# Local attention and channel mix in one kernel: GpSimd left out of tile arithmetic in the first units, one unit's scores split by tile, a longer strict list for TensorE

## The chip, the cores and the metric

The kernel runs on one core of a Trainium2 chip. The metric is the device time of one execution in microseconds (us); the figure for a kernel is the median of its runs. Beside the timed runs one execution is recorded by the hardware profiler; its span goes from the first to the last instruction of the program, and its own device time is a little longer.

Engines go by the profile's short names: PE is TensorE's matmul side and PEld its weight load, DVE is VectorE, ACT is ScalarE, POOL is GpSimd, SP is the engine whose queue issues all DMAs here. "L666" is line 666 of the kernel before.

## What is computed

A chunked local attention over 4 batches, 8 heads, 768 positions and 64 elements a head is followed by a channel mix over the 512 joined channels. All in fp32:

```python
for c in range(nc):                      # 24 chunks of 32 queries
    ...
    k_full = np.concatenate([mem_k, k_ctx], axis=2)   # 8 memory keys + 16 left + 32 + 8 right
    v_full = np.concatenate([mem_v, v_ctx], axis=2)
    scores = scale * np.matmul(q_c, k_full.transpose(0, 1, 3, 2))
    ...                                  # softmax over the 64 keys -> a
    out[:, :, c_start:c_end] = np.matmul(a, v_full)
...
xk = mu_k * x + (1.0 - mu_k) * x_prev    # x: attention output, x_prev: one position earlier
xr = mu_r * x + (1.0 - mu_r) * x_prev
k = np.maximum(xk @ w_k, 0.0)            # 512 -> 1024
v = k * k @ w_v                          # 1024 -> 512
r = 1.0 / (1.0 + np.exp(-(xr @ w_r)))    # 512 -> 512
return (r * v)
```

## The kernel before

**Tiling.** The 3072 positions are 24 tiles of 128 and 12 units of two tiles (256 positions). A unit u passes these steps on TensorE; each has a short name, used in the list below and in the text:

- `s u.c`: the scores, a matmul for each pair of heads, chunk and half (L371). Unit 0 does its two tiles as two operations (s0.0, s0.1); every other unit does both tiles as one, named s u.0. VectorE, ScalarE and VectorE again make the softmax of it: maximum (L384), subtraction (L389), exponential (L395), sum and reciprocal (L399 to L401), and the normalizing multiplication (L405).
- `t i`: four transposes of tile i's probabilities (L443). ScalarE or VectorE copies them into a block layout (L243 or L245).
- `a i`: the product with the values (L460). The result is copied into xT, the unit's transposed x.
- `h u.f`, four to a unit: xk times w_k (L666). For unit 0 these are eight "rows" instead, h0.k.c, one for each 128 rows k of w_k and each tile c (L641), so that each can start when its piece of w_k has come.
- `g u.c`: xr times w_r, one for each tile (L592; L584 for unit 0), followed by the sigmoid.
- `v u.c.half`: k squared times w_v (L740; L729 for unit 0), followed by the multiplication with the sigmoid (L762) and the store of the output (L765).

From unit 1 on, the channel mix splits each fp32 factor into a rounded high part (`xh`, `kh`, the weight tiles) and a low part (`xl`, `kl`, `wl`), and multiplies high by high, high by low and low by high. Unit 0 multiplies whole fp32 words. The low part of a weight is `T["w"] - high`, L299, one instruction on 128 x 1024 elements, once for each of ten weight pieces (4 of w_k, 2 of w_r, 4 of w_v). The low part of an input is L568. Before them stands the mixing: the difference of neighbouring positions (`df`, L542), then for m = 1 (gate) and m = 0 (w_k) four multiply-adds on 128 x 256 elements (L552).

**The order of the work.** The whole kernel is written as a list of operations (`Op`), each with one or several engines on which it may run, what it depends on, the buffer slots that it takes and uses, and a due time. `te_order` turns the string `LEAD` and, after it, a regular pattern for each unit into a sequence for TensorE with due times; `dues` passes due times back to all operations that these depend on. `turn` then places operations one after another on the engine and at the time where one can start first; due times break ties and, from the second turn on, weigh a tenth. `order` does three turns; each takes as its goals the starts that the turn before it gave. While fewer than `STRICT` operations of all engines are placed, TensorE may take only the next of its sequence; after that it may take a later one if that can start earlier. The loop at the end writes the instructions in the planned order, so on the chip each engine takes its instructions in that order; warm-up matmuls (L790) fill TensorE's planned pauses ahead of the first key row.

An operation with alternatives is made with `either`, such as `either(dve=(1.15, True), pool=(2.4, True))`; the numbers are planned costs, and the flag marks operations that are planned never to overlap between VectorE and GpSimd ("port"). GpSimd stands as an alternative in the normalizing multiplication (L415), the weights' low part (L309), the difference (L544), the input's low part (L573), the squaring (L707) and the low part of the square (L712).

**Buffers that matter here.** Score tiles and raw weights share five SBUF buffers ("big"), value tiles have two ("vw"); in PSUM there is one buffer for scores, two for transposes and value products ("tp") and four for the channel mix ("m"). A load into such a buffer is issued on SP's queue when its last user is done.

Of the kernel before, what the change touches and what calls it, by code (L numbers as in the profile page):

```python
# [27 lines left out]
NEG = -3.0e38  # L28
TINY = 2.0**-112
LOOK = 400  # L30
STRICT = 80
EASE = 0.1
TURNS = 3
LEAD = "s0.0 s0.1 t0 t1 a0 a1 h0.0.0 h0.0.1 h0.1.0 h0.1.1 s1.0 h0.2.0 h0.2.1 h0.3.0 h0.3.1 g0.0 t2 t3 g0.1 a2 a3 v0.0.0 s2.0 v0.0.1 v0.1.0 v0.1.1 h1.0 h1.1 h1.2 h1.3 g1.0 g1.1 t4 t5 a4 a5"
UTOK = 256
QPU = UTOK // P
QKW = NPAIR * NJ * (CHUNK + NK)
# [41 lines left out]
class Plan:  # L79
# [5 lines left out]
        self.bufs = bufs  # L85

    def op(self, alts, fn, deps=(), new=(), use=(), due=1e9):
        if isinstance(alts, tuple):
            alts = [alts]
        o = Op([(a + (False,))[:3] for a in alts], fn, deps, new, use, due)  # L90
        o.seq = len(self.ops)
        self.ops.append(o)
        return o

# [95 lines left out]
def local_attention__then__channel_mix(  # L190
# [47 lines left out]
    op = plan.op  # L238
    T = {}
# [4 lines left out]
        else:  # L244
            e.tensor_copy(dst, src)  # L245

    def either(**alts):
        return [(n, *alts[n]) for n in alts]

    qts = [(b, i) for b in range(B) for i in range(NQT)]  # L250
    units = [(b, u * UTOK) for b in range(B) for u in range(S // UTOK)]
# [1 line left out]
    due = te_order()  # L253
# [76 lines left out]
    xslot, pslot = {}, {}  # L330
    NG = 2 * QPU * NPAIR

    def scores(u):


        ts = range(u * QPU, (u + 1) * QPU)
        es = Slot("e")

        def grid(a, c, n):
            return a.rearrange("p (h c r) k -> p h c r k", h=2, c=QPU)[:, :, c : c + n].rearrange(  # L340
                "p h c r k -> p h (c r) k"
            )

        def f_load(t):
            b, i = qts[t]
            a = T["qk", t] = sb("big", [P, QKW], f"qk{t}")
            nc.sync.dma_start(a, qk[b, i])

        def part(c, n, prev, first):


            cs = range(c, c + n)
            G = NPAIR * n
            key = (u, c)

            def s4():
                return T["s", key].rearrange("p (h g k) -> p h g k", h=2, k=NK)[:, :, :G]

            def f_s():
                T["s", key] = ps("s", f"s{u}_{c}", QPU)  # L360
                s5 = s4().rearrange("p h (c r) k -> p h c r k", c=n)
                nq = NPAIR * NJ * CHUNK
                for d in cs:
                    a = T["qk", ts[d]]
                    q4 = a[:, :nq].rearrange("p (r j q) -> p r j q", r=NPAIR, j=NJ)
                    k4 = a[:, nq:].rearrange("p (r j k) -> p r j k", r=NPAIR, j=NJ)
                    for r in range(NPAIR):
                        for j in range(NJ):
                            for h in range(2):
                                z = slice(64 * h, 64 * h + 64)  # L370
                                nc.tensor.matmul(  # L371
                                    s5[CHUNK * j : CHUNK * (j + 1), h, d - c, r, :], q4[z, r, j, :], k4[z, r, j, :],
                                    start=True, stop=True,
                                )

            def f_max():
                s5 = s4().rearrange("p h (c r) k -> p h c r k", c=n)
                for d in cs:
                    if qts[ts[d]][1] == 0:
                        nc.vector.memset(s5[0:CHUNK, :, d - c, :, 0:LEFT], NEG)  # L380
                    if qts[ts[d]][1] == NQT - 1:
                        nc.vector.memset(s5[P - CHUNK : P, :, d - c, :, LEFT + CHUNK : LEFT + CHUNK + RIGHT], NEG)
                mx = T["mx", key] = sb("sm", [P, 2, G], f"mx{u}_{c}")
                nc.vector.reduce_max(mx, s4(), axis=AX.X)  # L384

            def f_sub():
                if first:
                    T["e", u] = sb("e", [P, NG, NK], f"e{u}")
                nc.vector.tensor_sub(  # L389
                    grid(T["e", u], c, n), s4(), T["mx", key].unsqueeze(3).to_broadcast([P, 2, G, NK])  # L390
                )

            def f_exp():
                e = grid(T["e", u], c, n)
                nc.scalar.activation(e, e, AF.Exp, scale=SCALE)  # L395

            def f_sum():
                sm = T["sum", key] = sb("sm", [P, 2, G], f"sum{u}_{c}")
                nc.vector.reduce_sum(sm, grid(T["e", u], c, n), axis=AX.X)  # L399
                nc.vector.tensor_scalar_add(sm, sm, 1e-9)  # L400
                nc.vector.reciprocal(sm, sm)  # L401

            def f_norm(g):
                e = grid(T["e", u], c, n)
                g.tensor_mul(e, e, T["sum", key].unsqueeze(3).to_broadcast([P, 2, G, NK]))  # L405

            w = n / QPU
            s1, m1, m2 = Slot("s"), Slot("sm"), Slot("sm")
            ds = due["s", u, c]
            o_s = op(("pe", 0.1 + 1.5 * w), f_s, [l[d] for d in cs] + [prev], new=[s1], use=[qs[d] for d in cs], due=ds)  # L410
            o_m = op(("dve", 0.1 + 1.05 * w), f_max, [o_s], new=[m1], use=[s1], due=ds + 4)
            o_b = op(("dve", 0.1 + 1.05 * w), f_sub, [o_m], new=[es] if first else [], use=[s1, m1] + [es] * (not first), due=ds + 5.5)
            o_e = op(("act", 0.15 + 0.85 * w), f_exp, [o_b], use=[es])
            o_u = op(("dve", 0.5 + 1.05 * w), f_sum, [o_e], new=[m2], use=[es])
            o_n = op(either(dve=(0.1 + 1.05 * w, True), pool=(2.2 * w, True)), f_norm, [o_u], use=[es, m2])  # L415
            if u == 0 and c == QPU - 1:
                prior["abs"].deps.append(o_e)
                prior["join"].deps.append(o_n)
            return o_s, [o_n] * n

        qs = [Slot("big") for _ in ts]
        l = [op(("dma", 2.1), lambda t=t: f_load(t), new=[x]) for t, x in zip(ts, qs)]
        o_s, done = prior.get("s"), []
        step = 1 if u == 0 else QPU
        for c in range(0, QPU, step):
            o_s, o_n = part(c, step, o_s, c == 0)
            done += o_n
        prior.update(s=o_s)
        return done, es
# [105 lines left out]
    def prep(u):  # L535
# [5 lines left out]
            d = T["df", u] = sb("x4", [P, KT, UTOK], f"df{u}")  # L541
            e.tensor_sub(d, x[:, :, 1:], x[:, :, :UTOK])  # L542

        o_d = op(either(dve=(1.15, True), pool=(2.0, True)), f_df, deps, new=[ds], use=[xslot[u]])  # L544
        for m in (1, 0):
            last = m == 0

            def f_mix(m=m, last=last):
                d = T["df", u]
                f = T["xf", u, m] = d if last else sb("x4", [P, KT, UTOK], f"xf{u}")  # L550
                for k in range(KT):
                    nc.vector.scalar_tensor_tensor(  # L552
                        f[:, k], d[:, k], mu_sb[:, m, k : k + 1], T["xT", u][:, k, :UTOK], ALU.mult, ALU.add
                    )

            def laid(m=m):
                f = T["xf", u, m]
                return f if m else f.rearrange("p k (n t) -> p t k n", t=2)

            shape = [P, KT, UTOK] if m else [P, 2, KT, UTOK // 2]  # L560

            def f_hi(e, m=m, laid=laid, shape=shape):
                h = T["xh", u, m] = sb(f"xh{m}", shape, f"xh{u}_{m}", F32R)
                copy(e, h, laid())

            def f_lo(e, m=m, laid=laid, shape=shape):
                l = T["xl", u, m] = sb(f"xl{m}", shape, f"xl{u}_{m}", F32R)
                e.tensor_sub(l, laid(), T["xh", u, m].bitcast(F32))  # L568

            fs, hs, ls = ds if last else Slot("x4"), Slot(f"xh{m}"), Slot(f"xl{m}")  # L570
            o_d = op(("dve", 1.75, True), f_mix, [o_d, o_mu], new=[] if last else [fs], use=[ds, xslot[u]])
            o_h = op(either(act=(0.97,), dve=(0.61, True)), f_hi, [o_d], new=[hs], use=[fs])
            o_l = op(either(dve=(1.15, True), pool=(2.4, True)), f_lo, [o_h], new=[ls], use=[fs, hs])  # L573
            mix[u, m] = (o_h, o_l, hs, ls)

    def channel_mix(u):
# [81 lines left out]
        for f in range(FT // 2):  # L658
# [45 lines left out]
                dh = due["h", u, f]  # L704
                o1 = op(("pe", BLOCK), f_s1, list(mix[u, 0][:2]) + wdeps(wk_hl, range(KT)), new=[s], use=list(mix[u, 0][2:]), due=dh)
            oa = op(either(act=(0.5,), dve=(0.61,)), f_relu, [o1], new=[kf], use=[s], due=dh + BLOCK + 1.5)
            ob = op(either(act=(0.54,), dve=(0.62, True), pool=(1.23, True)), f_sq, [oa], use=[kf])  # L707
            if is_whole(u, "v"):
                ks.append((ob, None, kh, kh))
                continue  # L710
            o2 = op(either(act=(0.54,), dve=(0.35, True)), f_hi, [ob], new=[kh], use=[kf])
            o3 = op(either(dve=(0.62, True), pool=(1.23, True)), f_lo, [o2], new=[kl], use=[kf, kh])  # L712
            ks.append((o2, o3, kh, kl))

        for c in range(QPU):
# [68 lines left out]
    with tc.manual_schedule():  # L784
        for o in plan.order():
            if o.eng == "pe":
# [2 lines left out]
                    warm = warm or ps("m", "warm")  # L789
                    nc.tensor.matmul(warm[:, :P], zero_sb, zero_sb, start=True, stop=True)  # L790
                busy = o.end
            if len(o.alts) > 1:
                o.fn(engines[o.eng])
            else:
                o.fn()
# [48 lines left out]
```

## Time and profile before

| what | value |
|---|---|
| median of 3 runs | 403.51 us (403.37 to 405.76) |
| the profiled execution's own time | 403.4 us |
| its span | 401.6 us |
| TensorE busy in the span | 393.3 us, 4506 matmul instructions |
| VectorE, ScalarE, GpSimd busy | 264.3, 189.1, 8.8 us |
| read from HBM, written | 42.01 MB, 6.29 MB |
| granted TensorE clock | 1.00 |

How to read it: a busy TensorE in the profile includes the warm-up matmuls and modelled ends of pipelined matmuls. An fp32 matmul appears as two matmul instructions. Timeline rows show the start, the length from the first to the last instruction of a merged group, the engine, the line, the tiles written and read, the count, and in brackets the idle time before the group and what ended it; "issue" there means that the profile shows nothing that the engine waited for. In a table by stage each engine's busy time in that stage is followed by its instruction count in brackets. A row of a DMA queue shows packets, megabytes, and the packets' time as a share of 16 engines' time in the window.

### The profile page before, as it was taken

Reading aid. Unit: us, or ns where it says so; the run is one execution under the profiler, and the core shown is the slowest. Engines: PE = TensorE matmul, PEld = TensorE weight load, DVE = VectorE, ACT = ScalarE, POOL = GpSimd, SP = SyncE. Lnnn points to the kernel's source line nnn. Section 1 sums busy time; section 2 is a strip of 40 time slices with the busy share of each in tenths; the row PEclk is TensorE's granted clock in tenths of the full one; section 3 lists DMA queues with packets and bytes.
Section 4 is the critical chain, followed back from the end, with each engine's and each line's share of the span. In section 5 each row is a group of like instructions: output and inputs, shape, how many; then the busy total and the mean of one; then the engine's idle time right before and its main releaser. Section 6 shows DMA issues by size and latency. Waiting matters only on the chain.

```text
span 401.6 us, 9978 instructions
## 1 busy us (share of the span) xinstructions
PE 393.3 (98%) x4506; PEld 352.0 (88%) x4506; DVE 264.3 (66%) x378; ACT 189.1 (47%) x271; POOL 8.8 (2%) x15
## 2 busy tenths in 40 slices
PE   8989998999999999999999999999999999999996
PEld 8988546988988998998998998998998998998995
DVE  2899899876396397397297288288378378377121
ACT  1657978661534435436436346255254354342250
POOL 2100130000000000000000000000000000000000
PEclk9999999999999999999999999999999999999999
DMA  8999925520052042133134134132130120100101
GB/s 317 421 368 387 414 95 205 243 106 26 28 192 98 28 155 113 52 124 141 52 112 154 52 107 158 54 107 80 54 106 2 54 105 3 54 2 0 52 2 52
DMA packets 12905, 48.93 MB, mean 122 GB/s; under 512 B 1472, under 2 KB 1600, under 8 KB 12352
## 3 DMA queue, kind: packets, MB, share of 16 engines
q1 hardware_dynamic: 12864, 48.31, 32.0%
q8 instruction: 35, 0.57, 0.6%
q14 instruction: 6, 0.05, 0.0%
HBM read 42.01 MB, written 6.29 MB: 120 GB/s over the span
## 4 chain that ended last, share of the span: by engine, by line
PE 95%; DVE 4%; issue 1%
PE ph L666 29%; PE pv L740 29%; PE pr L592 14%; PE px L460 6%; PE s L371 4%; PE ph L641 4%; PE warm L790 3%; PE pt L443 2%; PE pv L729 2%; PE pr L584 2%; DVE wl L299 1%; DVE xl L568 1%; DVE o L762 0%; DVE df L552 0%; DVE mx L384 0%
## 5 line engine op out<-in xcount | busy, mean ns | idle before, releaser
L666 PE MATMUL ph<-xh,wk 128*128 128x256 f32 x352 | 98.5, 280 | 0.0
L666 PE MATMUL ph<-xl,wk 128*128 128x256 f32 x352 | 96.8, 275 | 0.0
L666 PE MATMUL ph<-xh,wl 128*128 128x256 f32 x352 | 96.8, 275 | 0.0
L681 ACT ACTIVATE kf<-ph 128x512 f32<-128x512 f32 x39 | 23.1, 598 | 98.8 <-PE ph L666 98.8
L666 PEld LDWEIGHTS ph<-xh,wk 128*128 128x128 f32 x352 | 67.5, 192 | 1.0
L666 PEld LDWEIGHTS ph<-xl,wk 128*128 128x128 f32 x352 | 67.5, 192 | 0.3
L740 PE MATMUL pv<-wv,kh 128*128 128x512 f32 x176 | 67.7, 384 | 0.0
L666 PEld LDWEIGHTS ph<-xh,wl 128*128 128x128 f32 x352 | 67.6, 192 | 0.0
L740 PE MATMUL pv<-wl,kh 128*128 128x512 f32 x176 | 66.7, 379 | 0.0
L740 PE MATMUL pv<-wv,kl 128*128 128x512 f32 x176 | 66.7, 379 | 0.0
L698 DVE TENSOR_TENSOR kl<-kf,kh 128x512 fp32r<-128x512 f32 x44 | 29.5, 688 | 51.5 <-ACT kh L243 51.5
L762 DVE TENSOR_TENSOR o<-pv,sg 128x512 f32<-128x512 f32 x24 | 16.6, 691 | 37.8 <-PE pv L740 34.2
L740 PEld LDWEIGHTS pv<-wv,kh 128*128 128x128 f32 x176 | 33.3, 189 | 5.0
L740 PEld LDWEIGHTS pv<-wv,kl 128*128 128x128 f32 x176 | 33.3, 189 | 4.7
L740 PEld LDWEIGHTS pv<-wl,kh 128*128 128x128 f32 x176 | 33.3, 189 | 4.2
L592 PE MATMUL pr<-wr,xl 128*128 128x512 f32 x88 | 33.5, 380 | 0.4 <-DVE xl L568 0.4
L592 PE MATMUL pr<-wl,xh 128*128 128x512 f32 x88 | 33.4, 380 | 0.0
L592 PE MATMUL pr<-wr,xh 128*128 128x512 f32 x88 | 33.4, 379 | 0.0
L243 ACT CAST xh<-df 128x1024 fp32r<-128x1024 f32 x9 | 13.7, 1522 | 29.0 <-DVE df L552 29.0
L460 PEld LDWEIGHTS px<-aTz,vw 128*64 128x64 f32 x768 | 23.5, 138 | 2.8 <-issue 1.0
L460 PE MATMUL px<-aTz,vw 128*64 128x64 f32 x768 | 25.2, 224 | 0.4 <-issue 0.4
L245 DVE COPY aTz<-pt 64x512 f32<-64x512 f32 x21 | 14.6, 694 | 16.2 <-ACT aTz L243 10.9
(66 smaller groups left out, 566.2 us busy)
## 6 DMA issues: line engine op xcount, KB each, us to landing
qk<-in_qk_dram SPq DMA_DIRECT2D x24, 768.0 KB, 5.8
vw<-in_vw_dram SPq DMA_DIRECT2D x24, 512.0 KB, 4.8
out_dram<-o SPq DMA_DIRECT2D x24, 256.0 KB, 2.0
raw<-in_w_k_dram SPq DMA_DIRECT2D x4, 1024.0 KB, 9.8
raw<-in_w_v_dram SPq DMA_DIRECT2D x4, 1024.0 KB, 10.1
raw<-in_w_r_dram SPq DMA_DIRECT2D x2, 1024.0 KB, 7.7
id_sb<-in_ident_dram SPq DMA_DIRECT2D x1, 64.0 KB, 5.5
mu_sb<-in_mu_dram SPq DMA_DIRECT2D x1, 4.0 KB, 11.8
```

Source lines behind the costliest of these rows:

```text
L243: e.copy(dst, src)
L245: e.tensor_copy(dst, src)
L371: nc.tensor.matmul(s5[CHUNK * j : CHUNK * (j + 1), h, d - c, r, :], q4[z, r, j, :], k4[z, r, j, :], start=True, stop=True,)
L460: nc.tensor.matmul(p3[64 * h : 64 * h + 64, 2 * g : 2 * g + 2, CHUNK * j : CHUNK * j + CHUNK], v[:, g, h, j, :], a[:, h, g, j, :], start=True,
L592: nc.tensor.matmul(pairs(p), x[:, k, c * P : (c + 1) * P], woven(w), start=(k + n == 0), stop=(k == KT - 1 and n == 2),)
L641: nc.tensor.matmul(p[:, i * UTOK + c * P : i * UTOK + (c + 1) * P], T["w", id(wk_hl[0]), k][:, fc], T["xf", u, 0][:, k, z], start=(i + k + ...
L666: nc.tensor.matmul(pairs(p[:, i * UTOK : (i + 1) * UTOK]), w[:, fc], x[:, :, k].rearrange("p t n -> p n t"), start=(k + n == 0), stop=(k = ...
L681: e.activation(r, T["ph", u, f], AF.Relu)
L698: e.tensor_sub(l, T["kf", u, f], T["kh", u, f].bitcast(F32))
L740: nc.tensor.matmul(pairs(p), x[:, tc_], woven(w), start=(f + n == 0), stop=(f == FT - 1 and n == 2))
L762: nc.vector.tensor_mul(o, p, sg)
L790: nc.tensor.matmul(warm[:, :P], zero_sb, zero_sb, start=True, stop=True)
```

## The change

1. `either` leaves GpSimd out unless its first argument is true; the five uses within units give `u > 2`, and the weights' low part (L309) gives nothing. An operation that now has one engine left is still told which engine that is (`fixed`).
2. Unit 1's scores become two TensorE operations, one for each tile. Both write the same PSUM buffer; the softmax behind them stays one piece for both tiles.
3. `LEAD` is changed: s1.0 goes one key row earlier, s1.1 follows behind the next row; t4 and t5 go from behind g1.1 to between h1.1 and h1.2, a4 and a5 to between h1.2 and h1.3.
4. `STRICT` goes from 80 to 230 placed operations.

```diff
-STRICT = 80
+STRICT = 230
...
-LEAD = "s0.0 s0.1 t0 t1 a0 a1 h0.0.0 h0.0.1 h0.1.0 h0.1.1 s1.0 h0.2.0 h0.2.1 h0.3.0 h0.3.1 g0.0 t2 t3 g0.1 a2 a3 v0.0.0 s2.0 v0.0.1 v0.1.0 v0.1.1 h1.0 h1.1 h1.2 h1.3 g1.0 g1.1 t4 t5 a4 a5"
+LEAD = "s0.0 s0.1 t0 t1 a0 a1 h0.0.0 h0.0.1 h0.1.0 s1.0 h0.1.1 s1.1 h0.2.0 h0.2.1 h0.3.0 h0.3.1 g0.0 t2 t3 g0.1 a2 a3 v0.0.0 s2.0 v0.0.1 v0.1.0 v0.1.1 h1.0 h1.1 t4 t5 h1.2 a4 a5 h1.3 g1.0 g1.1"
...
     def op(self, alts, fn, deps=(), new=(), use=(), due=1e9):
-        if isinstance(alts, tuple):
+        fixed = isinstance(alts, tuple)
+        if fixed:
             alts = [alts]
...
-        o.seq = len(self.ops)
+        o.seq, o.fixed = len(self.ops), fixed
...
-    def either(**alts):
-        return [(n, *alts[n]) for n in alts]
+    def either(late=False, **alts):
+        return [(n, *alts[n]) for n in alts if n != "pool" or late]
...
-            def f_s():
-                T["s", key] = ps("s", f"s{u}_{c}", QPU)
+            def f_s(ds):
+                if ds[0] == c:
+                    T["s", key] = ps("s", f"s{u}_{c}", QPU)
...
-                for d in cs:
+                for d in ds:
...
-            o_s = op(("pe", 0.1 + 1.5 * w), f_s, [l[d] for d in cs] + [prev], new=[s1], use=[qs[d] for d in cs], due=ds)
+            o_s = prev
+            for g in [[d] for d in cs] if u == 1 else [list(cs)]:
+                first_s = g[0] == c
+                o_s = op(
+                    ("pe", 0.1 + 0.75 * len(g)), lambda g=g: f_s(g), [l[d] for d in g] + [o_s],
+                    new=[s1] * first_s, use=[s1] * (not first_s) + [qs[d] for d in g], due=due["s", u, g[0]],
+                )
...
-            o_n = op(either(dve=(0.1 + 1.05 * w, True), pool=(2.2 * w, True)), f_norm, [o_u], use=[es, m2])
+            o_n = op(either(u > 2, dve=(0.1 + 1.05 * w, True), pool=(2.2 * w, True)), f_norm, [o_u], use=[es, m2])
...
-            if len(o.alts) > 1:
+            if not o.fixed:
                 o.fn(engines[o.eng])
             else:
                 o.fn()
```

The uses at L544, L573, L707 and L712 get `u > 2` in the same way as the normalizing multiplication.

More of the change, by code (lines that the diff above doesn't have):

```diff
@@ L542, in f_df @@
             e.tensor_sub(d, x[:, :, 1:], x[:, :, :UTOK])
-        o_d = op(either(dve=(1.15, True), pool=(2.0, True)), f_df, deps, new=[ds], use=[xslot[u]])
+        o_d = op(either(u > 2, dve=(1.15, True), pool=(2.0, True)), f_df, deps, new=[ds], use=[xslot[u]])
         for m in (1, 0):
@@ L572, in prep @@
             o_h = op(either(act=(0.97,), dve=(0.61, True)), f_hi, [o_d], new=[hs], use=[fs])
-            o_l = op(either(dve=(1.15, True), pool=(2.4, True)), f_lo, [o_h], new=[ls], use=[fs, hs])
+            o_l = op(either(u > 2, dve=(1.15, True), pool=(2.4, True)), f_lo, [o_h], new=[ls], use=[fs, hs])
             mix[u, m] = (o_h, o_l, hs, ls)
@@ L706, in channel_mix @@
             oa = op(either(act=(0.5,), dve=(0.61,)), f_relu, [o1], new=[kf], use=[s], due=dh + BLOCK + 1.5)
-            ob = op(either(act=(0.54,), dve=(0.62, True), pool=(1.23, True)), f_sq, [oa], use=[kf])
+            ob = op(either(u > 2, act=(0.54,), dve=(0.62, True), pool=(1.23, True)), f_sq, [oa], use=[kf])
             if is_whole(u, "v"):
@@ L711, in channel_mix @@
             o2 = op(either(act=(0.54,), dve=(0.35, True)), f_hi, [ob], new=[kh], use=[kf])
-            o3 = op(either(dve=(0.62, True), pool=(1.23, True)), f_lo, [o2], new=[kl], use=[kf, kh])
+            o3 = op(either(u > 2, dve=(0.62, True), pool=(1.23, True)), f_lo, [o2], new=[kl], use=[kf, kh])
             ks.append((o2, o3, kh, kl))
```

## The prediction

> **What bounds the kernel now.** I read the top of the page first, then the span cut into stages, and last the timeline around each wait of TensorE.
>
> ```profile
> span 401.6 us, 9978 instructions
> PE 393.3 (98%) x4506; PEld 352.0 (88%) x4506; DVE 264.3 (66%) x378; ACT 189.1 (47%) x271; POOL 8.8 (2%) x15
> ```
> ```profile
> core 0: us, PE busy (x) PEld busy (x) DVE busy (x) ACT busy (x) POOL busy (x), PEclk, DMA share, GB/s
> 0.00:18.60 18.60, 16.91 (x282) 15.84 (x282) 10.35 (x21) 7.29 (x11) 3.54 (x10) 1.00 0.90 364
> 18.60:27.99 9.39, 9.39 (x197) 9.06 (x196) 8.73 (x17) 6.05 (x14) 0.00 (x0) 1.00 0.99 397
> 27.99:29.27 1.28, 0.00 (x0) 0.00 (x0) 1.28 (x3) 0.70 (x1) 0.00 (x0) 1.00 0.79 218
> 29.27:61.40 32.13, 32.13 (x309) 19.69 (x308) 29.47 (x37) 25.70 (x33) 4.98 (x2) 1.00 0.76 300
> 61.40:69.20 7.80, 6.36 (x165) 5.54 (x165) 7.80 (x8) 6.22 (x9) 0.00 (x0) 1.00 0.49 164
> 69.20:401.60 332.40, 328.53 (x3558) 301.88 (x3556) 206.68 (x298) 143.17 (x207) 0.32 (x3) 1.00 0.23 82
> ```
> TensorE is the bound. Up to 18.6 us it mostly passes time with warm-up matmuls; after that it works without a gap, but for one gap of 1.28 us and 1.44 us in the stage from 61.40 (the 3.87 us missing in the last stage lie behind its last matmul). Its clock is 1.00 throughout. The change moves TensorE's instructions and takes none away, so what can be won after 18.6 us is about 1.28 + 1.44 = 2.7 us, 0.7% of the span. The waits stand in brackets in the timeline (start, duration, engine, line); in the stage from 61.40 there are two:
>
> ```profile
> 48.54 5.06 POOL L299 TENSOR_TENSOR wl<-w,wk 128x1024 fp32r<-128x1024 f32 x2 [30.79 <-ACT wk L243]
> 48.88 5.79 DVE L552 SCALAR_TENSOR_TENSOR xf<-df,mu_sb,xT 128x256 f32<-128x256 f32 x4
> 51.00 10.57 PE L729 MATMUL pv<-w,kf 128*128 128x512 f32 x24
> 57.30 1.66 DVE L552 SCALAR_TENSOR_TENSOR df<-df,mu_sb,xT 128x256 f32<-128x256 f32 x4
> 61.24 1.22 DVE L405 TENSOR_TENSOR e<-e,sum 128x1024 f32<-128x1024 f32 x1
> 62.38 1.22 DVE L299 TENSOR_TENSOR wl<-w,wk 128x1024 fp32r<-128x1024 f32 x1
> 62.61 1.07 PE L443 MATMUL pt<-id_sb,e 128*128 128x128 f32 x8 [1.03 <-DVE e L405]
> 63.51 1.22 DVE L568 TENSOR_TENSOR xl<-df,xh 128x1024 fp32r<-128x1024 f32 x1
> 64.65 1.22 DVE L299 TENSOR_TENSOR wl<-w,wk 128x1024 fp32r<-128x1024 f32 x1
> 65.78 0.69 DVE L762 TENSOR_TENSOR o<-pv,sg 128x512 f32<-128x512 f32 x1
> 68.80 0.48 PE L592 MATMUL pr<-wr,xl 128*128 128x512 f32 x1 [0.40 <-DVE xl L568]
> ```
> Both of TensorE's waits there are for VectorE: the transposes t4 and t5 wait 1.03 us for unit 2's normalized softmax (L405), then the gate product g1.0 waits 0.40 us for the low part of its input (L568). The same four mixing instructions of VectorE take 5.79 us while GpSimd subtracts, and 1.66 us when it doesn't. So the two subtractions that GpSimd took over hold VectorE up by 5.79 - 1.66 = 4.13 us, and VectorE then has no rest until both of TensorE's waits are over (7.80 of 7.80 us busy from 61.40 on).
>
> **The change part by part.** *GpSimd.* Its 15 instructions hold only two on whole tiles, the two at L299 above; the others are fills and one small scaling. So taking it off the list for units 0 to 2 and for the weights moves these two and nothing else. On VectorE such a one follows the last after 1.13 us (62.38 to 63.51): it gains 4.13 us and takes on 2 x 1.13 = 2.26, and is free 1.87 us earlier from the mixing on. For TensorE that is worth at most its two waits. The norm would end at about 62.4 - 1.9 = 60.5, ahead of 61.58 (62.61 - 1.03), when the value product is done: 1.03 us gone. The gate's input is ready at 68.75 - 1.87 = 66.9, and TensorE, 1.03 us earlier, asks for it at 68.40 - 1.03 = 67.4: 0.40 us gone. Without any new order this part gives -1.43 us; the "fixed" flag and the alternatives that were never taken cost nothing.
>
> *The strict list.* TensorE now goes from the value product straight to h1.0 and h1.1, then t4, t5, h1.2, a4, a5, h1.3, g1.0, g1.1, v1.0.0, s3.0, g2.0. Its step lengths (start, duration, count; h and g stand in pairs):
>
> ```profile
> 99.66 5.36 PE ph L666 x48
> 108.57 2.02 PE px L460 x64
> 113.46 2.59 PE pv L740 x12
> 116.06 1.41 PE s L371 x89
> 120.26 5.18 PE pr L592 x24
> ```
> At 61.6 h1.0 must have four low parts of w_k and its input's two parts. VectorE's work for it, from 48.88: two mixings (2 x 1.66), four subtractions (4 x 1.13) and the input's low part (1.13), 9.0 us, to about 57.9, if the list's earlier dates put these ahead of unit 2's softmax: 3.7 us of cover. The softmax follows: max, subtract, exponential, sum and norm stand in the present trace between 54.90 and 62.4 with 1.58 and 0.61 us of other work inside, 5.3 us; from 57.9 it is done by about 64, and t4 comes at 61.6 + 5.36 = 67.0. g1.0 comes at 61.6 + 10.72 + 1.0 + 2.0 = 75.3, with three more operations (3.4 us) to do. Last, g2.0 needs unit 2's mixed input:
>
> ```profile
> 81.84 2.09 PE L460 MATMUL px<-aTz,vw 128*64 128x64 f32 x64
> 89.07 1.23 DVE L568 TENSOR_TENSOR xl<-xf,xh 128x1024 fp32r<-128x1024 f32 x1
> 83.03 1.26 SPq L437 DMA_DIRECT2D vw<-in_vw_dram  x2
> 66.94 2.06 SPq L347 DMA_DIRECT2D qk<-in_qk_dram  x4
> ```
> Today that is ready at 90.3, 6.4 us after a5 ends at 83.9. In the new list a5 ends at 72.6, and g2.0 comes at 75.3 + 5.2 + 2.6 + 1.4 = 84.5, so 11.9 us are there for 6.4. The cover gone, TensorE would wait one for one. Queued behind a blocked head are all of its later matmuls, and the output stores behind those; up to its 230th placed operation no other TensorE step may step in. Of the DMAs, the loads at L437 reuse the buffers of a4 and a5 and go out some 11 us earlier on SP's queue, for steps at 108.57; s3.0, moved from 63.6 to about 83, gives its two buffers back 20 us later, so part of the L347 loads comes then, for s4.0 at 116. With 32 us for a load that takes 13.6 us at the worst (next fence), nothing waits. The list is worth nothing on top of the 1.43 us.
>
> *The second unit's scores.* Their rows and the gap behind them:
>
> ```profile
> 18.63 7.41 PE L641 MATMUL ph<-xf,w 128*128 128x128 f32 x64
> 25.97 1.48 PE L371 MATMUL s<-qk 64*32 64x64 f32 x128
> 27.39 0.60 PE L641 MATMUL ph<-xf,w 128*128 128x128 f32 x3
> 29.27 6.97 PE L641 MATMUL ph<-xf,w 128*128 128x128 f32 x61 [1.28 <-issue]
> ```
> ```profile
> q8 instruction: 35, 0.57, 0.6%
> ...
> q8 instruction: 1, 0.02, 33.5%
> ...
> qk<-in_qk_dram SPq DMA_DIRECT2D x1, 768.0 KB, 13.6
> ```
> ```profile
> raw<-in_w_r_dram SPq DMA_DIRECT2D x1, 1024.0 KB, 7.8
> ```
> The gap lies inside a key row, with no new operand. I read it as instruction delivery: 2 x 4506 instructions came in 35 packets (the page's first q8 row), 257 each; and in the window from 26.8 to 27.0 stands the second q8 row, a packet that takes 33.5% of 16 x 0.2 us, 1.07 us, and so lands at about 28, as the gap begins. At key rows TensorE uses 122 instructions in 6.97 us; the scores use 256 in 1.48. That is inferred, not shown. The tile-wise split puts a key row (1.85 us) between the halves. The two tiles' loads (issued from 7.01, 13.6 us to landing) are there at 20.6 and some 2 us later, ahead of the new 24.1. But the instructions ahead of the gap's place are the same in either order, so TensorE gets there at 27.99 either way; only the request can go out earlier. If it goes out when TensorE comes to the block's first instruction, 8 instructions into the scores (26.0), it now comes 40 into them (24.1 + 40 x 1.48/256 = 24.3), 1.7 us earlier, and the 1.28 us are gone. If it goes out 40 or more instructions ahead, nothing moves: 0. The bad end: a block that takes as long as the data then in flight, 7.8 us, lands at 32.1, a gap of 4.1 us, 2.8 more than now. So -1.28 to +2.8; I take half of the gain, -0.6, since the packet of today came quickly and nothing slower is seen to be asked for. The Trainium skill ("Runtime: NRT & Kernel Launch", Instruction fetch mechanics) says that blocks of 256 instructions are fetched while the present one runs and that this is hidden, since an engine issues more slowly than the blocks come; the block size agrees with the rows, "hidden" would leave the gap another cause, and the sum would then be -1.43, 402.0 us.
>
> *Sum*, against the profiled execution's own 403.4 us (span 401.6 and 1.8 around it; the median of the runs is 403.51, 0.1 above): 403.4 - 1.03 - 0.40 - 0.6 = 401.4 us.
>
> **The rivals.** (1) The wait moves to h1.0: VectorE still serves unit 2's softmax ahead of the four subtractions and the input's low part. Present order with new costs: done at 65.8 - 4.13 + 2.26 = 63.9; h1.0 reads the last w_k part at its 12th of 24 matmuls, 1.2 us after 61.6, so TensorE waits 1.1 us at the head of a list that lets neither t4 nor s3.0 by. For it speaks that VectorE does the softmax first today; against it that the list gives h1.0 the earlier date. 403.4 - 1.43 + 1.1 = 403.1 us. (2) Slower: the instruction block asked for in the middle of the scores stands behind data transfers; place: the first matmuls after s1.1; price: up to 2.8 us. It decides from a landing at 29.27 + 1.43 = 30.7 us on. For it: DMA share 0.99 in that stage, and 7.8 us for data; against it: today's packet. 403.4 - 1.43 + 2.8 = 404.8 us. (3) The change does not do what it says on TensorE's side: the waits go through GpSimd's two instructions alone and the gap stays, 402.0 us; this lies in the forecast's own range. (4) The front shortens as well: up to 18.6 us TensorE has slack, but the list's first nine entries are the same, so I see no step that would.
>
> **How the numbers follow.** Forecast with both VectorE waits gone, 400.7 (whole gap gone) to 402.0 (gap stays): 0.63. Rival 1: 0.15. Rival 2: 0.15, of which 0.06 is for delays several times as long, past 1%. Rival 4: 0.07, mostly small. The range reaches from 400.5, just under the forecast's best, to 404.4, most of rival 2. About 1%, 4 us, is what a measurement of this kernel can tell from no change: the most that the trace has to give is 2.7 us, so faster by over 1% needs rival 4: 0.04; slower by over 1%: 0.06; within: 0.90.
>
> **What would show it right or wrong.** Right: GpSimd without L299; every four instructions at L552 in about 1.66 us; TensorE without a wait from 61 to 85 us, h1.0 right behind the value product; the last matmul some 2 us earlier. The gap behind the scores shorter or gone confirms the half taken; unchanged at 1.28 us, the sum is 402.0. Wrong: a wait of ph L666 for wl or xl (rival 1), a longer gap at L641 or between the halves of L371 (rival 2), a wait of g2.0 for xl, or a first key row that no longer starts near 18.6 us.

## The result and the profile after

The changed kernel takes 401.73 us (median of 6 runs), the kernel before beside it 403.89 us; the ratio of the two is 0.9938, with a 95% interval from 0.9918 to 0.9957. That is 2.2 us or 0.6% faster, and within the 1% that the prediction set as its bound. The profiled execution took 401.57 us against 403.4, 1.8 us less; the account below is made on it. One of the six runs of experiment x3 below took 671.6 us at a granted clock of 0.558, against 0.998 or more in its other five, and is left out of its ratio.

The top of the page, and the stages up to 69.20 us, cut where this kernel has its gap and its waits would be:

```profile
span 399.8 us, 9971 instructions
...
PE 392.7 (98%) x4506; PEld 352.1 (88%) x4506; DVE 263.3 (66%) x381; ACT 188.7 (47%) x270; POOL 3.4 (1%) x13
```
```profile
0.00:18.60 18.60, 16.54 (x282) 15.42 (x282) 10.44 (x21) 7.29 (x11) 3.04 (x10) 1.00 0.91 363
18.60:28.35 9.75, 9.71 (x195) 9.21 (x196) 8.78 (x17) 6.65 (x14) 0.00 (x0) 1.00 1.00 391
28.35:29.43 1.08, 0.00 (x0) 0.00 (x0) 1.08 (x2) 0.29 (x1) 0.00 (x0) 1.00 0.96 387
29.43:61.70 32.27, 32.27 (x311) 20.02 (x311) 29.67 (x38) 26.02 (x33) 0.00 (x0) 1.00 0.83 316
61.70:69.20 7.50, 7.50 (x70) 7.50 (x69) 7.07 (x9) 5.23 (x8) 0.00 (x0) 1.00 0.68 247
```
GpSimd has two instructions less, and TensorE is busy throughout the stage from 61.70, where it lacked 1.44 us. The gap behind unit 1's scores is still there, with 1.08 us. The timeline of VectorE and TensorE (start, duration, engine, line; L560 is the old L552, L300 the old L299, L451 the transposes, L649 the key rows, L373 the scores, L674 the old L666):

```profile
49.03 1.67 DVE L560 SCALAR_TENSOR_TENSOR xf<-df,mu_sb,xT 128x256 f32<-128x256 f32 x4
...
57.76 2.48 DVE L300 TENSOR_TENSOR wl<-w,wk 128x1024 fp32r<-128x1024 f32 x2
...
64.26 1.22 DVE L407 TENSOR_TENSOR e<-e,sum 128x1024 f32<-128x1024 f32 x1
```
```profile
18.63 5.62 PE L649 MATMUL ph<-xf,w 128*128 128x128 f32 x48 [0.41 <-DVE xf L533]
24.19 0.86 PE L373 MATMUL s<-qk 64*32 64x64 f32 x64
24.98 2.05 PE L649 MATMUL ph<-xf,w 128*128 128x128 f32 x16
26.96 0.86 PE L373 MATMUL s<-qk 64*32 64x64 f32 x64
27.75 0.60 PE L649 MATMUL ph<-xf,w 128*128 128x128 f32 x3
29.43 6.97 PE L649 MATMUL ph<-xf,w 128*128 128x128 f32 x61 [1.09 <-issue]
...
66.90 1.04 PE L451 MATMUL pt<-id_sb,e 128*128 128x128 f32 x8
```
The four mixing instructions take 1.67 us instead of 5.79. The last low part of w_k is ready at 60.24 and the softmax at 65.48; TensorE needs them at about 62.8 and 66.9.

From the chain that ended last, the start of unit 2's h2.0, up to which both kernels have done the same work (before: 99.66, in the prediction):

```profile
97.84 5.36 PE ph L674 x48
```
So 1.82 us are won by then, the whole of it. The path up to the end of the gap became longer: the first key row starts at 18.63 in both, and the gap ends at 29.43 instead of 29.27. From there to h2.0 it is 68.41 us instead of 70.39, 1.98 us less. Most of that, 1.77 us, is the two waits for VectorE, as x1 shows below; the other 0.21 us come with the new order of the steps.

### The profile page after: what moved, and what is told of

The parts are those of the page before. It is cut to its first block, busy times and chain, and to the rows that moved or that the text cites. A ratio compares the mean times of both kernels' runs of the same rounds, so it can differ in the third digit from the quotient of the medians.

```text
span 399.8 us, 9971 instructions
## 1 busy us (share of the span) xinstructions
PE 392.7 (98%) x4506; PEld 352.1 (88%) x4506; DVE 263.3 (66%) x381; ACT 188.7 (47%) x270; POOL 3.4 (1%) x13
## 4 chain that ended last, share of the span: by engine, by line
PE 94%; DMA 3%; SPq 1%; ACT 0%; issue 0%; DVE 0%; DVEq 0%
PE ph L674 30%; PE pv L748 29%; PE pr L600 14%; PE px L468 6%; PE s L373 4%; PE ph L649 4%; PE pv L737 4%; DMA raw<-in_w_k_dram 3%; PE pt L451 2%; PE pr L592 2%; ACT w L286 0%; SPq L445 0%; SPq L348 0%; SPq L270 0%; DVE o L770 0%
## 5 line engine op out<-in xcount | busy, mean ns | idle before, releaser
L674 PE MATMUL ph<-xh,wk 128*128 128x256 f32 x352 | 99.0, 281 | 0.0
L674 PE MATMUL ph<-xl,wk 128*128 128x256 f32 x352 | 96.8, 275 | 0.0
L674 PE MATMUL ph<-xh,wl 128*128 128x256 f32 x352 | 96.8, 275 | 0.0
L674 PEld LDWEIGHTS ph<-xh,wk 128*128 128x128 f32 x352 | 67.5, 192 | 1.2 <-issue 0.2
L674 PEld LDWEIGHTS ph<-xl,wk 128*128 128x128 f32 x352 | 67.5, 192 | 0.5 <-DVE e L391 0.2
L674 PEld LDWEIGHTS ph<-xh,wl 128*128 128x128 f32 x352 | 67.6, 192 | 0.0
L397 ACT ACTIVATE e<-e 128x1024 f32<-128x1024 f32 (+1 forms) x13 | 12.9, 993 | 28.5 <-DVE e L391 28.5
```

What stands on the lines that cost most here:

```text
L674: nc.tensor.matmul(pairs(p[:, i * UTOK : (i + 1) * UTOK]), w[:, fc], x[:, :, k].rearrange("p t n -> p n t"), start=(k + n == 0), stop=(k = ...
```

## The experiments

Ten kernels. Each ratio is to the kernel before on the same chip and comes from the timed runs; a span is that of the one profiled execution, and spans of one kernel's runs differ by up to 1.1 us in most of these kernels and by 2.2 to 4.0 us in four (x3, y2, y3, y4).

| kernel | span, us | ratio (95% interval) |
|---|---|---|
| the changed kernel | 399.8 | 0.9938 (0.9918 to 0.9957) |
| x1, only the engine of two instructions | 400.0 | 0.9956 (0.9944 to 0.9968) |
| x2, changed, GpSimd back | 400.7 | 0.9969 (0.9957 to 0.9981) |
| x3, changed, wide warm-up | 398.7 | 0.9920 (0.9902 to 0.9937) |
| x4, changed, scores in one piece | 400.1 | 0.9946 (0.9934 to 0.9958) |
| y1, changed, two warm-up matmuls fewer | 400.0 | 0.9952 (0.9938 to 0.9967) |
| y2, before, wide warm-up | 402.6 | 1.0006 (0.9991 to 1.0022) |
| y3, GpSimd out, old list | 400.8 | 0.9974 (0.9959 to 0.9990) |
| y4, wide warm-up, one piece, t later | 399.1 | 0.9931 (0.9915 to 0.9948) |
| z1, y4 with two operations exchanged | 398.9 | 0.9912 (0.9899 to 0.9926) |
| z2, the new list alone | 401.2 | 0.9972 (0.9961 to 0.9982) |

**x1: only the engine of the two subtractions.** Every engine keeps its old order.

```diff
-                o.fn(engines[o.eng])
+                o.fn(engines["dve" if o.eng == "pool" else o.eng])
```


> The kernel before with every engine's order as it was; only the two subtractions at L299 that GpSimd did go to VectorE, at their old places in the plan. Theory A (VectorE's lateness, made by GpSimd, is what TensorE waited for): the four mixing instructions at L552 take 1.66 us again, the norm is ready by 60.6 us and the gate's input by 67, both of TensorE's waits are gone although its sequence is the old one, the gap of 1.28 us stays, span 401.6 - 1.8 = 399.8 us. Rival B (the new sequence is what wins): in the old sequence the waits stay within 0.3 us of 1.03 and 0.40, span 401.3 to 401.6 us.

Measured: 400.0 us. VectorE, then TensorE's first waits on its list of waits:

```profile
49.16 1.67 DVE L552 SCALAR_TENSOR_TENSOR xf<-df,mu_sb,xT 128x256 f32<-128x256 f32 x4
...
59.67 1.23 DVE L405 TENSOR_TENSOR e<-e,sum 128x1024 f32<-128x1024 f32 x1
```
```profile
PE ph L641 <- issue: 1.2, 1, 1.2
PE warm L790 <- DVE zero_sb L232: 1.0, 1, 1.0
PE px L460 <- POOL xT L472: 0.4, 1, 0.4
```
Both waits for VectorE are gone in the old sequence. What they cost is the time from the gap's end to h2.0, in the chain that ended last (the second row is cut by the view's end at 100 us):

```profile
29.49 6.97 PE ph L641 x61
98.11 1.90 PE ph L666 x17
```
That is 68.62 us instead of 70.39, so 1.77 us, for listed idle times of 1.43. The span falls by 1.6 us only, because here the first key row starts 0.3 us later (18.89 us instead of 18.63), though the instructions ahead of it are the same. Theory A holds and B falls: two instructions on another engine are worth 0.44%, against 0.62% for the whole change, and the two intervals overlap.

**x2: the changed kernel with the two subtractions on GpSimd.**

```diff
+    slow = [wdone[id(wk_hl[0]), k][1] for k in range(2)]
...
-                o.fn(engines[o.eng])
+                o.fn(engines["pool" if o in slow else o.eng])
```


> The changed kernel in its own order, but its first two low parts of w_k go back to GpSimd. Theory A: the first four mixing instructions take about 5.8 us again, VectorE is late by 4.13 - 2.26 = 1.9 us, h1.0 still finds its operands (about 62.1 us against 62.9 us), the softmax for t4 is late (about 67.4 against 66.9 us), so one wait of 0.5 us at t4 and a span of about 400.4 us. Rival B (the sequence carries the gain, VectorE's time doesn't matter): 399.8 us, no wait. Rival C (GpSimd alone carries it and the sequence hides nothing): 401.5 us, with waits of 1.4 us or more.

Measured: 400.7 us. VectorE's mixing and TensorE's wait:

```profile
49.07 5.77 DVE L560 SCALAR_TENSOR_TENSOR xf<-df,mu_sb,xT 128x256 f32<-128x256 f32 x4
```
```profile
PE pt L451 <- DVE e L407: 0.8, 1, 0.8
```
The 5.8 us are back, h1.0 doesn't wait, t4 waits 0.8 us (expected 0.5). So the new sequence hides a part of VectorE's lateness, and B and C both fall.

**z2: the new list and the strict count alone.**

```diff
-STRICT = 80
+STRICT = 230
...
-LEAD = "... v0.1.1 h1.0 h1.1 h1.2 h1.3 g1.0 g1.1 t4 t5 a4 a5"
+LEAD = "... v0.1.1 h1.0 h1.1 t4 t5 h1.2 a4 a5 h1.3 g1.0 g1.1"
```


> The kernel before with the new list and the strict count of 230 alone (scores in one piece, GpSimd allowed as before; the planner then gives GpSimd other work: one input's low part, one low part of w_r, one low part of a square, 2.5 us each or less). Theory A (what counts is whether VectorE is held up ahead of TensorE's needs): GpSimd's work comes later, where the list leaves more time, so part of the two waits stays: span 400.0 to 401.0 us. Rival B (the list alone carries the gain): 399.8 us. Rival C (GpSimd's removal alone does): 401.3 us or more.

Measured: 401.2 us, a little above A's range and just under C's; this execution was one of the longest of its eight, whose median span of 400.9 us lies in A's range. The gap has 1.9 us here instead of 1.3, and t4 waits 0.7 us. The plan now gives GpSimd other work, and VectorE is held up again, a subtraction of 1.22 us taking 3.39:

```profile
56.90 2.54 POOL L568 TENSOR_TENSOR xl<-xf,xh 128x1024 fp32r<-128x1024 f32 x1 [39.62 <-ACT xh L243]
```
```profile
57.13 3.39 DVE L568 TENSOR_TENSOR xl<-df,xh 128x1024 fp32r<-128x1024 f32 x1
```
GpSimd's subtraction ends at 59.44 and VectorE's at 60.52, 1.08 us later, about what it takes alone. The list alone is worth 0.28% (1.1 us). From the gap's end (29.95) to h2.0 (99.28) it is 69.33 us: the list without GpSimd's removal wins 1.06 of the 1.98 us there.

**y3: GpSimd's removal alone, as written,** with the planner free to reorder: the `either` and `fixed` hunks of the change, nothing else.

> The kernel before with the change's first part alone, as written: GpSimd is no alternative in units 0 to 2, list and strict count as before; the planner then also finds another order on TensorE by itself. Theory A: no wait for VectorE is left, the gap stays, span 399.8 us. Rival B (the new list carries the gain): 401.3 us or more.

Measured: 400.8 us, a miss by 1.0 for A, though no wait for VectorE's softmax or low parts is left. The planner put t4 and t5 between and behind the gate products with a4 right after them, which costs a new wait (a4 for a copy, 0.3 us), the first key row starts some 0.3 us later, and the gap is 1.7 us. This run doesn't separate the theories well; x1, with the order held, does.

**x4: the changed kernel with unit 1's scores in one piece.**

```diff
-            for g in [[d] for d in cs] if u == 1 else [list(cs)]:
+            for g in [[d] for d in cs] if u == -1 else [list(cs)]:
...
-LEAD = "... h0.1.0 s1.0 h0.1.1 s1.1 h0.2.0 ..."
+LEAD = "... h0.1.0 h0.1.1 s1.0 h0.2.0 ..."
```


> The changed kernel with unit 1's scores in one piece at the old place, the rest as changed. Theory A with D: the gap comes back to about 1.28 us (0.2 more), but a switch into the scores and one out of them less save about 0.36 us; span 399.6 us, that is the split costs 0.15 us. Rival F (the split is worth its half of the gap, as the prediction took it): 400.4 us.

Measured: 400.1 us and 0.9946. The gap is 1.5 us, and the key rows start about 0.3 us later. Against the changed kernel's 0.9938 that is no difference that these intervals can tell: neither the 0.15 us that I expected the split to cost nor F's 0.6 us gain is shown.

**x3: the changed kernel with wide warm-up matmuls.** As many microseconds of warm-up, in half as many instructions, to move the border between instruction blocks.

```diff
-    zero_sb = const.tile([P, P], F32, tag="zero", name="zero_sb")
+    zero_sb = const.tile([P, 2 * P], F32, tag="zero", name="zero_sb")
...
-                n = 0 if ("ph", 0, 0) in T else int((o.start - busy - 0.2) / (0.22 if busy else 0.43))
+                n = 0 if ("ph", 0, 0) in T else int((o.start - busy - 0.2) / (0.44 if busy else 0.86))
...
...
-                    nc.tensor.matmul(warm[:, :P], zero_sb, zero_sb, start=True, stop=True)
+                    nc.tensor.matmul(warm[:, : 2 * P], zero_sb[:, :P], zero_sb, start=True, stop=True)
```


> The changed kernel; the warm-up matmuls ahead of the first key row are 256 columns wide and half as many, so that TensorE is as long busy with about 84 instructions fewer ahead of the scores. Theory D (the gap behind the scores is TensorE out of instructions at the border of a block of about 256): the border moves some 84 instructions, 4.8 us of key rows, behind its old place, and the gap of 1.09 us is gone or under 0.2 us, span 398.7 us. Rival E (the gap belongs to its place: a late operand or a full buffer there): the gap stays at the fourth matmul of h0.2.0 with about 1.1 us, span 399.8 us.

Measured: 398.7 us. The key rows behind the scores now run through, 64 in one row:

```profile
27.16 0.86 PE L373 MATMUL s<-qk 64*32 64x64 f32 x64
27.95 7.41 PE L649 MATMUL ph<-xf,w 128*128 128x128 f32 x64
```
D holds and E falls.

**y1: the changed kernel with two warm-up matmuls fewer.**

```diff
-                for _ in range(n):
+                for _ in range(n - 2 * (n > 11)):
```


> The changed kernel with two of its 41 warm-up matmuls left out (8 instructions with their loads), all else the same. Theory D (end of an instruction block): the gap moves 8 instructions further into the key row, from behind its 4th matmul instruction to behind its 8th, and is shorter by their time, 0.45 us: 0.6 to 0.7 us instead of 1.09; span 399.4 us. Rival E (the gap belongs to its place): behind the 4th instruction again, 1.1 us, 399.8 us.

Measured: 400.0 us. The gap stands behind 7 matmul rows instead of 3, exactly 8 instructions on:

```profile
18.92 5.62 PE L649 MATMUL ph<-xf,w 128*128 128x128 f32 x48
...
28.04 1.05 PE L649 MATMUL ph<-xf,w 128*128 128x128 f32 x7
30.11 6.52 PE L649 MATMUL ph<-xf,w 128*128 128x128 f32 x57 [1.03 <-issue]
```
Counted from the start, its place has not moved at all: ahead of the gap stand 477 matmul and 478 load instructions of TensorE in both kernels (the first two stages of the changed kernel's table add up to the same 955), and in all the others that have this gap. So the place is as D expected; the length isn't: 1.03 us instead of 0.65. The packet on the instruction queue comes later as well. Windows around it, first of the changed kernel (27.1 to 27.3), then of y1 (27.6 to 27.7):

```profile
q8 instruction: 1, 0.02, 31.3%
```
```profile
q8 instruction: 1, 0.02, 60.8%
```
In the kernel before the packet starts at about 26.9 and the gap ends at 29.27, in the changed one at about 27.1 and 29.43, in y1 at about 27.6 and 30.11: 2.3 to 2.5 us from the packet's start to the gap's end (2.6 in z2). Of the 0.5 us by which y1's packet is later, 0.3 lie ahead of the first key row (18.92 us instead of 18.63). What sets the packet's start is not shown.

**y2: the kernel before with wide warm-up alone.** The edit is x3's, on the kernel before.

> The kernel before with the wide warm-up matmuls alone, so that the gap of 1.28 us goes and nothing else changes. Theory A (TensorE then waits for VectorE, which is late by its own work): most of it is swallowed, the wait at t4 grows from 1.03 towards 2.3 us, span 401.0 to 401.6 us. Rival G (gap and waits add up): the wait at t4 stays at 1.0 us, span 400.3 us.

Measured: 402.6 us in the profile, 1.0006: no gain, as A said, but by another way. The gap behind the scores is gone (64 key rows in one row); then come ScalarE, whose rectification at L681 stands behind a weight's conversion (L285) that waits for its load, and TensorE behind it; and the moved border now lies in the middle of s3.0, with a packet in the window from 64.1 to 64.3 (its row stands in the last block below). Ahead of that gap stand 859 matmul and 859 load instructions, 763 more than the 955 of the others, or three blocks of about 254:

```profile
27.34 7.41 PE L641 MATMUL ph<-xf,w 128*128 128x128 f32 x64
36.03 3.70 PE L584 MATMUL pr<-w,xf 128*128 128x512 f32 x8 [1.27 <-ACT kf L681]
...
66.42 0.42 PE L371 MATMUL s<-qk 64*32 64x64 f32 x21 [1.46 <-issue]
```
```profile
34.37 1.13 ACT L285 ACTIVATE w<-raw 128x1024 f32<-128x1024 f32 x1 [2.38 <-DMA raw<-in_w_v_dram]
35.40 1.06 ACT L681 ACTIVATE kf<-ph 128x512 f32<-128x512 f32 x2
```
```profile
q8 instruction: 1, 0.02, 31.9%
q1 hardware_dynamic: 5, 0.00, 1.4%
```
The second row of the last block is the data traffic in that window: next to none, and TensorE still stalls for 1.46 us. So traffic beside the packet is not needed for such a gap.

So the gap hid a second wait. In x3, which has the split, that wait doesn't come. The split gives its first score buffer back earlier, and the first w_v load goes out at 25.08 us in the changed kernel (third row of its queue below) instead of 26.86 before. (The first rows show that a score load now goes ahead of a w_k load; the first key row starts at 18.63 us all the same.)

```profile
5.05 0.33 SPq L348 DMA_DIRECT2D qk<-in_qk_dram  x1
7.03 0.33 SPq L270 DMA_DIRECT2D raw<-in_w_k_dram  x1
...
25.08 3.14 SPq L272 DMA_DIRECT2D raw<-in_w_v_dram  x2
```
```profile
26.86 1.51 SPq L271 DMA_DIRECT2D raw<-in_w_v_dram  x2
```

**y4: a version to beat both:** x4 with wide warm-up, and in the list `h1.0 h1.1 h1.2 t4 t5 h1.3 a4 a5 g1.0 g1.1`.

> A version to beat both: the changed kernel with wide warm-up matmuls, unit 1's scores in one piece, and t4, t5 one step later (h1.0 h1.1 h1.2 t4 t5 h1.3 a4 a5 g1.0 g1.1). Theory A with D: no gap behind the scores, no wait at t4 (0.2 us with wide warm-up alone), two switches less (0.36 us): span 398.1 to 398.4 us. Rival: VectorE, with less time ahead of g2.0, is late there, a wait for xl of 0.5 us or more, span 398.7 us or above.

Measured: 399.1 us, above what I expected, and for neither reason named: without the split the wait at g0.0 is back, with 1.1 us.

```profile
35.52 3.70 PE L592 MATMUL pr<-w,xf 128*128 128x512 f32 x8 [1.11 <-ACT kf L689]
```

**z1: y4 with the rectifications ahead of the conversion.**

```diff
-        for o in plan.order():
+        todo = plan.order()
+        todo.remove(signs[6])
+        todo.insert(todo.index(relus[1]) + 1, signs[6])
+        for o in todo:
```
Here `signs[6]` is the conversion (L285) of the first w_v piece and `relus[1]` unit 0's second rectification.

> The version without the split, with wide warm-up and t4, t5 later, and one thing more: on ScalarE the first two rectifications of unit 0 (L681 in the kernel before) stand ahead of the conversion of the first w_v piece (L285), which waits for its load. Theory H (without the gap, TensorE waits at g0.0 for a rectification that is queued behind the late w_v load; the split hides this by giving a score buffer back earlier): the wait of 1.1 us at g0.0 goes, span 398.0 us. Rival I (g0.0 waits for something else that ends at the same time): a wait of 1 us at g0.0 stays, 399.1 us.

Measured: 398.9 us. The wait at g0.0 is gone, as H said; 15 us later, at s2.0, another has taken most of its place, for the scores' load:

```profile
PE s L375 <- DMA qk<-in_qk_dram: 0.7, 1, 0.7
```
So the profiled span falls by 0.2 us only, and 398.0 is missed; the ratios of y4 and z1 differ by 0.19% (0.8 us), with intervals that overlap. With 0.9912 (0.9899 to 0.9926) z1 and with 0.9920 (0.9902 to 0.9937) x3 are the fastest measured; between the two the intervals don't decide, and both overlap with the changed kernel's (0.9918 to 0.9957), whose span is 1.1 us longer than x3's and 0.9 us longer than z1's.

## Why the prediction was right, step by step

- **Time.** 401.4 us forecast, 401.73 measured, inside the range of 400.5 to 404.4 and within 1% as expected. That it came out so well is partly luck: in the profile 1.82 us were won of 2.03 forecast, the waits gave 1.77 instead of 1.43, the order 0.21 instead of nothing, and the scores cost 0.16 instead of winning 0.6.
- **GpSimd holds VectorE up by 4.13 us.** Right: the mixing takes 1.67 us without it, and 5.77 again in x2. The Trainium skill ("SBUF — State Buffer", Who interferes with whom) has the rule: a VectorE instruction with two SBUF inputs contends with a GpSimd instruction that reads SBUF, and the port pair that the two engines share is an exclusive lock. The traces agree, with 4.1 us in x2 and 2.2 us in z2. The plan had flagged both sides never to overlap (L309, and L571 for the mixing); in the trace of the kernel before they do all the same, GpSimd from 48.54 to 53.60 us and VectorE from 48.88.
- **The two waits, -1.43 us.** Mechanism right, shown by x1; the size was short: 1.77 us in x1. I had added the idle times. A wait costs more: the matmul that waits 0.40 us starts at 68.80 (last row of the prediction's first timeline), 0.78 us behind the one before it, where neighbours in its group are 0.22 us apart:

```profile
67.80 0.38 PE L592 MATMUL pr<-wr,xh 128*128 128x512 f32 x1
68.02 0.38 PE L592 MATMUL pr<-wl,xh 128*128 128x512 f32 x1
```
That is 0.56 us for a listed idle time of 0.40, since the record of a matmul (0.38 us) is longer than its step (0.22).

- **The strict list, worth nothing on top.** It is so far as the intervals reach: x1, without it, has 0.9956 and the change 0.9938. In the profiles it adds a little: 68.41 us from the gap's end to h2.0 instead of x1's 68.62, and 68.41 again in x4; why the new order is 0.21 us shorter with no wait in either is not shown. And it isn't idle: x2 and z2 show that it hides a part of VectorE's lateness if GpSimd stays. g2.0 didn't wait, nor did h1.0; rival 1 didn't come, as the earlier dates did put the low parts first.
- **The scores, -0.6 us.** This term failed. The gap fell by 0.19 us only (1.28 to 1.09), and the way to it became 0.36 us longer (first key row at 18.63 in both, the first instruction behind the scores at 27.75 instead of 27.39): one more switch into the scores and out of them. Together +0.16 us. For the gap itself the direction was right: the three kernels with the split and narrow warm-up have gaps of 1.03 to 1.12 us (changed, x2, y1), the five in one piece 1.24 to 1.87 (before, x1, x4, y3, z2), one profile each; but the longer way to it takes 0.36 us of that back. The cause that I inferred, an instruction block that comes late, is shown by x3 and y1. The step that failed is that the request goes out earlier by what TensorE gains: the packet came at about 27.1 us instead of 26.9. In both kernels it starts while TensorE works on the last 64 score matmuls ahead of the gap, and the split leaves these where they were; what sends the request out stays open. By the rule of the Trainium skill ("Runtime: NRT & Kernel Launch", Instruction fetch mechanics) that the fetch is hidden the gap would have had another cause; its move by exactly 8 instructions in y1 decides against that.
- **The moved loads, nothing waits.** Right for the change's time, but incomplete. I followed the loads that the list moves and not the buffer that the split gives back: it sends the first w_v load out 1.8 us earlier. That is worth nothing while the gap stands, and 1.1 to 1.3 us once it is closed (y2 and y4 against x3).

What stays open: what sets the time at which an instruction packet starts, and so why the gap has 1.2 to 1.9 us in five kernels with the same instructions up to there; and how much the new list adds to x1, 0.2 us by the profiles, for which the intervals are too wide.

## What to carry to other kernels

Where a helper engine takes work off a busy one, look at what the busy one does meanwhile: here two subtractions moved to GpSimd held VectorE up by 4.1 us and saved it 2.3. Count a wait by start-to-start times, not by the idle column. Before a gap is costed as a gain, look for the next wait behind it in the same stage: an engine that waits for a load with other work queued behind it will show only when the gap is closed.

## What the runs showed of the hardware

- TensorE stalled 1.0 to 1.9 us at borders between instruction blocks (9012 matmul and load instructions in 35 packets of 16 KB, about 257 each): behind 955 instructions in eight kernels, behind 1718 in y2. From the packet's start to the next matmul it was 2.2 to 2.6 us. The 256 instructions ahead of the border had been used up in 2.0 us in the kernel before and in 4.0 in the changed one. The stall moved 8 instructions within the work when 8 fewer stood ahead of it (y1) and vanished when some 84 fewer did (x3). In the stage ahead of it the DMA engines were busy at 0.99 in the kernel before and 1.00 in the changed one; in y2 it came with 1.4% of data traffic beside the packet.
- While GpSimd ran two subtractions of 128 x 1024 elements (5.06 us), four VectorE instructions on 128 x 256 elements took 5.79 us instead of 1.66.
- A matmul that resumes after a wait of 0.40 us by the record came 0.56 us late.
- Going into 64 score matmuls and back to key rows once more cost 0.36 us (9.12 us from the first key row to the first instruction behind the scores instead of 8.76; 9.11 in x3).
